# Attention with memory and a feed-forward stage on one core: the second group's maxima ahead of the block transpositions, phi behind the scalings, the next pair's fourth scores between two parts of the values

## The chip, the core and the metric

The kernel runs on one core of a Trainium2 chip. The metric is device time in microseconds (us). A core has engines that run side by side, each working through its own instructions in order: PE (TensorE) multiplies matrices (PEld is its loading of weights), DVE (VectorE), ACT (ScalarE) and POOL (GpSimd) work on elements, and SP issues most of the DMA transfers. PE has two clock levels, 1.2 and 2.4 GHz; the profile shows the granted level as a share of the full one.

## What is computed

```python
B, H, S, D = (4, 8, 576, 64)
scores = scale * np.matmul(q, k.transpose(0, 1, 3, 2))      # scale = 1/8
scores = np.where(causal, -1000000000.0, scores)
a = np.exp(scores - scores.max(-1, keepdims=True))
a /= a.sum(-1, keepdims=True) + 1e-09
local = np.matmul(a, v)
phi = lambda x: np.where(x > 0, x, np.exp(x) - 1.0) + 1.0
mem_out = einsum('bhsd,bhde->bhse', phi(q), M_prev) / (einsum('bhsd,bhd->bhs', phi(q), z_prev)[..., None] + 1e-06)
attn = g * mem_out + (1 - g) * local                         # g = sigmoid(beta), per head
x = attn.transpose(0, 2, 1, 3).reshape(B * S, H * D)         # 2304 x 512
h = x @ w_in                                                 # 512 x 2048
out = (h * sigmoid(1.702 * h)) @ w_out                       # 2048 x 512
```

All in float32. A product of the feed-forward stage is made of three passes of split numbers (high times high, low times high, high times low).

## The kernel before, in words

**Attention goes by pairs.** A pair is one batch and two heads; there are 16. The first four (batch 0) go through `plan_rest`, the other twelve through `plan_full`. Below they are full pairs 1 to 12. The change touches the full pairs, but for one line that also holds for the four.

**A full pair, in the order in which PE meets it.** The 576 rows of queries are four row blocks of 128 (i = 0 to 3) and a tail of 64. PE does, for one pair: the *fourth scores* (i = 3, four matmuls of 512 columns, tile `ps`, two PSUM banks); the *second group* (i = 2, 1, 0, tile `rows`, four banks); then the scores of the tail of the *next* pair together with the *early part* of the values (tile `po`, four banks: memory product from `qpt`, and keys from block 8 on); then the *late part* of the values (key blocks 0 to 7), behind which the fourth scores of the next pair stand. The four banks of `rows` and of `po` are the same PSUM: the early part cannot start before the last exponential has read `rows`, and the second group cannot start before the last subtraction `xl` has read `po`.

**Softmax of one row block.** DVE adds the mask and finds the maximum (line 642, called *maxima*; a second short instruction reads the accumulator), ACT does the exponential with its row sums (line 649, tile `a`), DVE adds the sums and takes the reciprocal (lines 732 and 733), POOL scales the rows (line 652), DVE transposes the block in 32 x 32 pieces into `eT` (line 860; the tail at lines 868 and 869). The early part waits for the transpositions of i = 3 and 2, the late part for those of i = 1 and 0.

**phi(q).** ACT makes exp of the negative part (lines 562 and 569), POOL takes the positive part and adds (line 577 and a tensor_tensor at helper line 168), multiplies with z (`qmt`), DVE sums (`nrm`, line 592) and takes the reciprocal, POOL multiplies (`qp<-qp,nrm`), DVE transposes (line 612, `qpt`, called *query transposition*). phi is made one pair ahead; its tile `qp` has one buffer, so the next phi waits for the query transposition.

**Values into the next stage.** ACT copies `po` into `xh`, DVE subtracts into `xl` (both at helper lines).

**Feed-forward blocks fill PE.** The first product is 128 blocks of twelve matmuls (tile `pm`, 256 or 320 columns, two PSUM banks in turn). ACT copies a finished block out (`hk`, line 160) and SP stores it to DRAM; a block can start only when its bank has been copied out. The second product (tile `acc`, line 1274) follows after all pairs.

**What sets the order.** `at(slot, prio, fn)` puts an emission into a slot with a priority, `feed` and `PACE` hand out blocks between, and a scheduler that simulates the time at build makes each engine's order from that. `tc.add_manual_dep(..., NOSYNC, ...)` only fixes an order on one engine; with SYNC it is a wait. `group` keeps its matmuls together and lets the first wait for what its list names. `behind_x` orders an instruction behind the last `xl`. `decode` puts one unpacking of output weights (three DVE instructions, lines 1102, 1103 and 1105, *bit operations*, behind one ACT scaling, line 1120) into most full pairs.

## Time and profile before

| | |
|---|---|
| median of 3 runs | 624.48 us (622.62 to 630.42) |
| profiled execution, its own time | 625.55 us |
| its span, first to last instruction | 623.8 us |
| mean granted clock of PE | 0.978 |
| busy: PE, DVE, ACT, POOL | 90%, 67%, 55%, 39% of the span |

PE is busy for nine tenths of the span, so the time is PE's work plus PE's idle time. The idle time lies at the start, where the first inputs arrive, and in the stretch of the pairs; from 400 us on PE is busy throughout. Of an engine that is not PE, only that idle time counts that PE waits for.

### The profile page before, as it was taken

How to read it: one execution, taken by the hardware profiler on the slowest of the kernel's cores; microseconds unless marked ns; L12 is line 12 of the kernel's file. 1: busy time of each engine (PE TensorE's matmuls, PEld its weight loads, DVE VectorE, ACT ScalarE, POOL GpSimd, SP SyncE). 2: the span in 40 equal slices, each digit the busy share in tenths (PEclk: the TensorE clock that was granted, in tenths of full speed). 3: DMA queues.
4: the chain of work that ended last, by engine and by line, in shares of the span. 5: the costliest groups of instructions: out<-in, count | busy, mean ns of one | idle time of the engine just before them, and what ended most of it. 6: DMA issues, size and time to landing. Idle time of an engine off the chain costs nothing.

```text
span 623.8 us, 17375 instructions
## 1 busy us (share of the span) xinstructions
PE 559.6 (90%) x6984; PEld 497.3 (80%) x6984; DVE 417.1 (67%) x993; ACT 343.1 (55%) x816; POOL 244.8 (39%) x326
## 2 busy tenths in 40 slices
PE   5799998987699787988898898799999999999997
PEld 4367776866577676876777798799999999999997
DVE  5788876647766555665755735957588569756964
ACT  5678785445535444464544523655676865666441
POOL 4757575557446337247346340240402301320000
PEclk9999999989989899999998999899999999999999
DMA  7976444545654554655642564422545823562002
GB/s 250 369 275 205 134 135 149 179 139 165 208 170 120 202 149 160 204 162 159 208 142 78 178 199 165 154 90 96 191 140 138 272 73 79 164 189 76 25 1 77
DMA packets 48736, 97.73 MB, mean 157 GB/s; under 512 B 5520, under 2 KB 33424, under 8 KB 48656
## 3 DMA queue, kind: packets, MB, share of 16 engines
q1 hardware_dynamic: 42416, 74.60, 37.1%
q0 software_dynamic: 6240, 22.02, 11.4%
q8 instruction: 55, 0.90, 0.6%
q14 instruction: 25, 0.20, 0.1%
HBM read 73.01 MB, written 23.59 MB: 155 GB/s over the span
## 4 chain that ended last, share of the span: by engine, by line
PE 33%; issue 10%; DVE 9%; POOL 4%; DMA 4%; ACT 3%; POOLq 0%; ACTq 0%; DVEq 0%
PE acc L1274 15%; PE pm L141 11%; PE po L141 5%; POOL g L1217 2%; DMA g<-gd 2%; DMA wraw<-in_w_out_dram 2%; PE ps L141 2%; POOL a L652 2%; DVE eT L860 1%; ACT a L649 1%; DVE ps L642 1%; DVE xl L168 1%; DVE rows L642 1%; DVE g L168 1%; DVE eT L868 1%
## 5 line engine op out<-in xcount | busy, mean ns | idle before, releaser
L141 PE MATMUL pm<-xh,wi 128*128 128x320 f32 (+1 forms) x1024 | 220.6, 309 | 19.9 <-ACT hk L160 16.2
L141 PEld LDWEIGHTS pm<-xh,wi 128*128 128x128 f32 x1024 | 169.5, 195 | 39.1 <-ACT hk L160 19.4
L1274 PE MATMUL acc<-oh,wo 128*128 128x384 f32 x672 | 169.9, 337 | 0.2 <-ACT oh L160 0.2
L141 PE MATMUL pm<-xl,wi 128*128 128x256 f32 (+1 forms) x512 | 154.0, 301 | 0.6 <-DVE xl L168 0.6
L1274 PEld LDWEIGHTS acc<-oh,wo 128*128 128x128 f32 x672 | 121.8, 188 | 0.5 <-ACT oh L160 0.5
L1274 PE MATMUL acc<-ol,wo 128*128 128x384 f32 x336 | 111.4, 338 | 0.2 <-DVE ol L168 0.2
L168 DVE TENSOR_TENSOR ol<-g,oh 128x768 fp32r<-128x768 f32 x84 | 79.9, 956 | 44.4 <-ACT oh L160 44.0
L141 PEld LDWEIGHTS pm<-xl,wi 128*128 128x128 f32 x512 | 99.9, 195 | 0.9 <-DVE xl L168 0.9
L160 ACT ACTIVATE oh<-g 128x768 fp32r<-128x768 f32 x84 | 69.9, 842 | 48.6 <-PE acc L1274 41.6
L652 POOL TENSOR_SCALAR a<-a,sm,g 128x512 f32<-128x512 f32 (+3 forms) x112 | 69.2, 629 | 44.5 <-DVE sm L733 34.0
L1217 POOL DMA_DIRECT2D g<-gd x48 | 34.8, 725 | 111.7 <-DVE ol L168 65.5
L160 ACT ACTIVATE hk<-pm 128x256 f32<-128x256 f32 (+1 forms) x113 | 45.5, 409 | 59.8 <-PE pm L141 47.4
L1274 PEld LDWEIGHTS acc<-ol,wo 128*128 128x128 f32 x336 | 63.0, 188 | 0.5 <-DVE ol L168 0.5
L141 PE MATMUL po<-eT,vr 32*64 32x64 f32 (+4 forms) x3072 | 53.5, 258 | 6.9 <-issue 6.9
L649 ACT ACTIVATE a<-rows,nm 128x256 f32<-128x256 f32 (+2 forms) x72 | 33.2, 473 | 45.2 <-DVE nm L642 33.4
L141 PE MATMUL ps<-kqf 64*64 64x512 f32 (+3 forms) x288 | 39.5, 547 | 20.1 <-DVE sm L733 13.8
L141 PEld LDWEIGHTS po<-eT,vr 32*64 32x64 f32 x3072 | 48.6, 136 | 10.2 <-issue 9.7
L860 DVE STREAM_TRANSPOSE eT<-a 128x1024 f32<-128x1024 f32 (+3 forms) x48 | 40.5, 843 | 18.4 <-POOL a L652 17.4
L168 POOL TENSOR_TENSOR qp<-qp,nrm 128x576 f32<-128x576 f32 (+1 forms) x16 | 17.2, 1074 | 85.2 <-DVE sm L733 83.6
L642 DVE CUSTOM_DVE_ANT_0 ps<-ps,mask 128x512 f32<-128x512 f32 (+3 forms) x72 | 38.1, 556 | 17.2 <-PE ps L141 16.4
L1223 ACT ACTIVATE g<-g 128x768 f32<-128x768 f32 x48 | 39.5, 838 | 13.6 <-DMA g<-gd 13.2
L168 DVE TENSOR_TENSOR g<-g,g 128x768 f32<-128x768 f32 x48 | 45.5, 953 | 1.4 <-ACT g L1223 1.4
(146 smaller groups left out, 750.2 us busy)
## 6 DMA issues: line engine op xcount, KB each, us to landing
g<-gd POOLq DMA_DIRECT2D x48, 384.0 KB, 4.8
vr<-in_vt_dram SPq DMA_DIRECT2D x24, 576.0 KB, 5.0
gd<-hk SPq DMA_DIRECT2D x64, 160.0 KB, 2.3
kqf<-in_kq_dram SPq DMA_DIRECT2D x12, 768.0 KB, 5.0
wraw<-in_w_in_dram SPq DMA_DIRECT2D x16, 512.0 KB, 5.7
gd<-hk SPq DMA_DIRECT2D x64, 128.0 KB, 2.0
wraw<-in_w_out_dram SPq DMA_DIRECT2D x10, 512.0 KB, 4.1
qr<-in_qt_dram SPq DMA_DIRECT2D x12, 288.0 KB, 3.1
```

The costliest lines, as they stand in the source:

```text
L141: x = nc.tensor.matmul(out, l, r, start=start, stop=stop)
L160: return nc.scalar.activation(out=dst, in_=src, func=AF.Copy, **kw)
L168: return (nc.vector if eng == "V" else nc.gpsimd).tensor_tensor(out=dst, in0=a, in1=b, op=op)
L642: x = nc.vector.tensor_tensor_reduce(out=ps, in0=ps, in1=mk, op0=ALU.add, op1=ALU.min, scale=-0.125, scalar=1e38 if j == 0 else nm[:, j - ...
L649: return nc.scalar.activation(out=a, in_=ps, func=AF.Exp, scale=-1.0, bias=nm, accum_out=sm)
L652: return (nc.vector if eng == "V" else nc.gpsimd).tensor_scalar(out=a, in0=a, scalar1=r, scalar2=gcol, op0=ALU.mult, op1=ALU.mult)
L860: x = nc.vector.transpose(out=blocks()[:, :4 * i + 4, i:9 - i:8 - 2 * i].rearrange("p k h n -> p h k n"), in_=U["a", i].rearrange("p h (k ...
L868: behind_x(nc.vector.transpose(out=e[:, :, 4], in_=a[:, :16]))
L1217: x = nc.gpsimd.dma_start(t, gd[4 * kh + p][:, :, t0:t0 + QN].rearrange("i p t -> p i t"))
L1223: x = nc.scalar.activation(out=t, in_=t, func=AF.Gelu_apprx_sigmoid)
L1274: nc.tensor.matmul(acc[b, j][:, :QN], W[2 * p + kk][:, WPART[i], sp, 128 * j:128 * j + 128], mv[:, kk], start=first and p + kk == 0 and sp ...
```

## The change

Five edits. (1) `a_blocks`: the transposition of i = 3 now stands on DVE behind the second group's maxima (`state["max"]`) and behind the reciprocal that was emitted last (`state["inv"]`), and those of i = 2, 1, 0 two slots later, behind the last reciprocal; they were in slots of their own, behind `xl` alone. (2) `qblocks`: the query transposition comes behind a reciprocal too. (3) `qphi`: POOL's positive part comes behind the last scaling emitted. (4) `products`: the late part is split into key blocks 4 to 7 and 0 to 3, and `first_group` puts the next pair's fourth scores between the two. (5) `exp_unit`: the exponentials of i = 3 stand on ACT behind the copy `xh`.

```diff
--- before.py
+++ after.py
@@ -574,7 +574,8 @@
             if rest:
                 nc.vector.scalar_tensor_tensor(out=qp, in0=qv(), scalar=0.0, in1=qm, op0=ALU.max, op1=ALU.add)
             else:
-                nc.gpsimd.tensor_scalar(out=qp, in0=qv(), scalar1=0.0, scalar2=None, op0=ALU.max)
+                x = nc.gpsimd.tensor_scalar(out=qp, in0=qv(), scalar1=0.0, scalar2=None, op0=ALU.max)
+                tc.add_manual_dep(x.ins, state["scaled"], NOSYNC, reason="not yet")
                 tt("P", qp, qp, qm, ALU.add)
 
         def zmul():
@@ -609,9 +610,11 @@
 
         def qblocks():
             t = P["qT"] = att.tile([128, 2, 9, 32], F32, name="qpt0", bufs=2)
-            P["qblocks"] = nc.vector.transpose(
+            x = nc.vector.transpose(
                 out=t.rearrange("p k s n -> p s k n"),
-                in_=P["qp"][:, :9].rearrange("p s (k n) -> p s k n", n=32)).ins.name
+                in_=P["qp"][:, :9].rearrange("p s (k n) -> p s k n", n=32))
+            tc.add_manual_dep(x.ins, state["inv"], NOSYNC, reason="not yet")
+            P["qblocks"] = x.ins.name
 
         steps = (qmin, qexp, qphi, zmul, norm, smul)
         if rest:
@@ -622,7 +625,7 @@
         else:
             times = (7, 7, 8, 9, 10, 11)
             at(s0 + 11, 53, mplain)
-            at(s0 + 12, 53, qblocks)
+            at(s0 + 12, 89.6, qblocks)
         for k, fn in zip(times, steps):
             at(s0 + k, 49 if fn is zmul else 53, fn)
         if p + 1 < len(pairs):
@@ -725,16 +728,19 @@
             used(U.get(("in", h, i), U["ps", h, i]), x)
             if i < 2:
                 behind_hk(x)
+            if i == 3 and "xh" in state:
+                tc.add_manual_dep(x.ins, state["xh"], NOSYNC, reason="not yet")
             U["exp", h, i] = state["exp"] = state["late A"] = x.ins.name
 
         def inv_unit(i):
             sm = U["rs", i] = sml.tile([128, 2], F32, name="sm")
             nc.vector.tensor_reduce(out=sm, in_=U["sm", i], op=ALU.add, axis=AX.X)
-            nc.vector.reciprocal(out=sm, in_=sm)
+            state["inv"] = nc.vector.reciprocal(out=sm, in_=sm).ins.name
 
         def scale_unit(h, i):
             hh = 2 * c + h
-            scale_rows(U["a", i][:, h], U["rs", i][:, h:h + 1], g1[:, hh:hh + 1])
+            x = scale_rows(U["a", i][:, h], U["rs", i][:, h:h + 1], g1[:, hh:hh + 1])
+            state["scaled"] = x.ins.name
 
         return max_unit, exp_unit, inv_unit, scale_unit
 
@@ -860,7 +866,8 @@
             x = nc.vector.transpose(
                 out=blocks()[:, :4 * i + 4, i:9 - i:8 - 2 * i].rearrange("p k h n -> p h k n"),
                 in_=U["a", i].rearrange("p h (k n) -> p h k n", n=32))
-            behind_x(x)
+            tc.add_manual_dep(x.ins, state["max"], NOSYNC, reason="not yet")
+            tc.add_manual_dep(x.ins, state["inv"], NOSYNC, reason="not yet")
             P["tr", i] = x.ins.name
 
         def t_blocks():
@@ -877,7 +884,7 @@
 
         def products():
             po, ms, ops = U["po"], P["ms"], []
-            for k in (-2, -1, *range(8, KB), *range(8)):
+            for k in (-2, -1, *range(8, KB), *range(4, 8), *range(4)):
                 for Q in range(4):
                     for h in range(2):
                         r, own = slice(32 * Q, 32 * Q + 32), h == Q // 2
@@ -893,9 +900,9 @@
                             ops.append((k, Q, h, i, 4 + own, w, slots(P["eT"], r, k, h, i, own)))
             last = {o[1:3]: n for n, o in enumerate(ops)}
 
-            def part(early):
+            def part(*ks):
                 for n, (k, Q, h, x, y, l, mv) in enumerate(ops):
-                    if early == (k < 0 or k >= 8):
+                    if k in ks:
                         dst = po[64 * h:64 * h + 64, Q, 32 * x:32 * y].rearrange("p (s n) -> p s n", n=32)
                         mm(dst, l, mv, k == -2, last[Q, h] == n)
                 state["pe"] += 0.5
@@ -921,7 +928,7 @@
                         parts.append((r, slice(256, CT), po[r, 2 * h:2 * h + 2, 128:160]))
                 for r, x, src in parts:
                     xh, xl = [t[r, c, x].rearrange("p (s n) -> p s n", s=src.shape[1]) for t in xq[n]]
-                    copy("A", xh, src)
+                    state["xh"] = copy("A", xh, src).ins.name
                     subs.append((xl, src, f32(xh)))
                 if c == NP - 1:
                     xplan[n] = state["slot"] + 1
@@ -943,15 +950,16 @@
                 fns.append(lambda: s_tail(p + 1, prep[p + 1]["tail"]))
             room()
             part = products()
-            group(fns + [lambda: part(True)], names)
-            values["next"] = (lambda: None, [lambda: part(False)], [P["tr", 1]])
+            group(fns + [lambda: part(-2, -1, *range(8, KB))], names)
+            values["next"] = (lambda: None, [lambda: part(*range(4, 8)), lambda: part(*range(4))], [P["tr", 1]])
 
         def first_group():
             late = values.pop("next", None)
             names, fns = (late[2], late[1]) if late else (rooms(KEEP), [])
             for h in range(2):
                 U["ps", h, 3] = U["in", h, 3] = bank("ps")
-            group(fns + [lambda: s_quads(p, 3, [U["ps", h, 3] for h in range(2)])], names)
+            fns.insert(1, lambda: s_quads(p, 3, [U["ps", h, 3] for h in range(2)]))
+            group(fns, names)
 
         def second_group():
             own = late_ps["rows"] = ExitStack()
@@ -980,7 +988,7 @@
                 at(x, (30, 29, 26, 25)[i], lambda h=h, i=i: exp_unit(h, i))
                 at(x + 1, 13 - i, lambda h=h, i=i: scale_unit(h, i))
             at(x, 91 - i, lambda i=i: inv_unit(i))
-            at(k0 + k + 3, 13 - i, lambda i=i: a_blocks(i))
+            at(k0 + (4 if i == 3 else 6), (18, 17, 16, 89.4)[i], lambda i=i: a_blocks(i))
         at(k0 + 7, 40, early_values)
         at(k0 + 7, 99, lambda: feed(1.0, True))
         if p + 1 == len(pairs):
```

Line numbers of the changed kernel are 1 to 8 higher from line 577 on (642 becomes 645, 652 becomes 655, 860 becomes 866).

On DVE, in full pair 9, from the reciprocal of i = 3 on (`rows` with 384, 256 and 128 columns are the maxima of i = 2, 1, 0; `eT<-a3` is the transposition of i = 3; `qpt0` that of the queries), before:

```order
L733 RECIPROCAL sm_4537<-sm_4537 128x2
L612 STREAM_TRANSPOSE qpt0_4648<-qp_4509 128x9x2x32
L860 STREAM_TRANSPOSE eT_4542<-a3_4531 128x2x16x32
L642 ISA rows_4578,nm_4619<-rows_4578,mask_145 128x384
L642 ISA nm_4619 128x1
L642 ISA rows_4579,nm_4621<-rows_4579,mask_145 128x384
L642 ISA nm_4621 128x1
L642 ISA rows_4580,nm_4623<-rows_4580,mask_145 128x256
```

and now, where the maxima of i = 2 follow the same reciprocal directly:

```order
L738 RECIPROCAL sm_4521<-sm_4521 128x2
L645 ISA rows_4548,nm_4589<-rows_4548,mask_145 128x384
L645 ISA nm_4589 128x1
...
L738 RECIPROCAL sm_4615<-sm_4615 128x2
L866 STREAM_TRANSPOSE eT_4526<-a3_4515 128x2x16x32
L613 STREAM_TRANSPOSE qpt0_4619<-qp_4493 128x9x2x32
L737 TENSOR_REDUCE sm_4621<-sum3_164 128x2
L738 RECIPROCAL sm_4621<-sm_4621 128x2
L737 TENSOR_REDUCE sm_4624<-sum4_165 128x2
L738 RECIPROCAL sm_4624<-sm_4624 128x2
L866 STREAM_TRANSPOSE eT_4526<-a2_4601 128x2x12x32
```

Both transpositions moved behind all six maxima, and the transposition of i = 2 behind the last two reciprocals. Before, the query transposition stood ahead of the maxima of i = 2 in ten of the twelve full pairs, and the transposition of i = 3 in seven of them (pairs 1, 5, 7 and 9 to 12) and between the maxima of i = 2 and 1 or 0 in the other five; now neither stands ahead of the maxima of i = 2 in any.

On POOL, in the same pair (`a3` and `a2` are scalings, `qp<-qr` is the positive part), before:

```order
L652 TENSOR_SCALAR a3_4531<-a3_4531,sm_4537,g1_158 128x512 x2
L577 TENSOR_SCALAR qp_4897<-qr_4233 128x576
L652 TENSOR_SCALAR a2_4631<-a2_4631,sm_4650,g1_158 128x384 x2
L652 TENSOR_SCALAR a2_4643<-a2_4643,sm_4653,g1_158 128x256 x2
L652 TENSOR_SCALAR a2_4643<-a2_4643,sm_4656,g1_158 128x128 x2
L168 TENSOR_TENSOR qp_4897<-qp_4897,qmt_181 128x576
```

and now:

```order
L655 TENSOR_SCALAR a2_4601<-a2_4601,sm_4615,g1_158 128x384 x2
L655 TENSOR_SCALAR a2_4610<-a2_4610,sm_4621,g1_158 128x256 x2
L655 TENSOR_SCALAR a2_4610<-a2_4610,sm_4624,g1_158 128x128 x2
L577 TENSOR_SCALAR qp_4881<-qr_4203 128x576
L168 TENSOR_TENSOR qp_4881<-qp_4881,qmt_181 128x576
L168 TENSOR_TENSOR qmt_181<-qp_4881,zb_4516 128x2x4x64
```

The positive part moved from ahead of six scalings to behind them.

On PE the scheduler also deals the blocks out anew. Matmuls of blocks (twelve to a block) that stand in each full pair between the late part with its fourth scores and the second group (A), and between the second group and the next tail scores (B), of 256 columns unless marked w (320 columns), as the order of the changed kernel has them:

| pair | 2 | 3 | 4 | 5 | 6 | 7 | 8 | 9 | 10 | 11 | 12 |
|---|---|---|---|---|---|---|---|---|---|---|---|
| A | 12w | 12w | 12w | 24 | 24 | 24 | 12w | 12w | 12 | 24 | 12 + 12w |
| B | 27w | 33w | 24w | 48 | 51 | 45w | 42w | 42w | 54 | 45 | 36w |

Between the early and the late part stand 0 to 18 matmuls of blocks in each pair, before and now. Over the twelve pairs 36 matmuls of 320 columns (three blocks) fewer stand among the pairs than before, and 36 more behind the last pair.

## Rows read from the trace of the kernel before

**Rows 1.** Stretches by time: busy us and count per engine, clock, DMA share, GB/s
```profile
104.00:362.00 258.00, 219.53 (x4494) 184.54 (x4491) 159.94 (x521) 122.87 (x398) 130.06 (x172) 0.95 0.53 164
362.00:443.00 81.00, 74.97 (x760) 73.64 (x745) 52.33 (x97) 38.79 (x73) 16.36 (x15) 0.98 0.41 140
```

**Rows 2.** PE's waits, 104 to 362 us: total us, times, longest
```profile
PE ps L141 <- DVE sm L733: 13.8, 5, 4.6
PE pm L141 <- ACT hk L160: 10.7, 10, 3.0
PE po L141 <- issue: 6.9, 6, 2.1
PE ps L141 <- issue: 2.9, 1, 2.9
PE rows L141 <- DVE xl L168: 1.9, 3, 0.6
PE ps L141 <- ACT hk L160: 1.4, 1, 1.4
```

**Rows 3.** The six stretches at half clock: sum of busy time, same columns
```profile
sum 23.88, PE 13.76 PEld 11.01 DVE 14.40 ACT 15.39 POOL 14.36; mean PE 2.29 PEld 1.83 DVE 2.40 ACT 2.57 POOL 2.39
```

**Rows 4.** Timeline of PE, full pair 9: start, us, instruction, [idle before]
```profile
273.31 2.27 PE L141 MATMUL po<-eT,vr 32*64 32x160 f32 x128
275.50 1.09 PE L141 MATMUL ps<-kqf 64*64 64x512 f32 x8
280.24 1.53 PE L141 MATMUL rows<-kqf 64*64 64x384 f32 x24
...
287.03 0.50 PE L141 MATMUL pm<-xh,wi 128*128 128x256 f32 x2 [1.56 <-ACT hk L160]
...
289.91 0.77 PE L141 MATMUL ps<-kqf 64*64 64x256 f32 x8
```

**Rows 5.** Timeline of DVE, full pair 9
```profile
275.63 0.69 DVE L1105 SCALAR_TENSOR_TENSOR r<-wraw,r 128x512 int32<-128x512 int32 x1
...
276.64 0.70 DVE L642 CUSTOM_DVE_ANT_0 ps<-ps,mask 128x512 f32<-128x512 f32 x1 [0.17 <-PE ps L141]
...
280.57 0.11 DVE L733 RECIPROCAL sm<-sm 128x2 f32<-128x2 f32 x1
281.93 0.78 DVE L612 STREAM_TRANSPOSE qpt<-qp 128x576 f32<-128x576 f32 x1 [1.25 <-POOL qp L168]
283.43 1.25 DVE L860 STREAM_TRANSPOSE eT<-a 128x1024 f32<-128x1024 f32 x1 [0.72 <-POOL a L652]
284.70 0.57 DVE L642 CUSTOM_DVE_ANT_0 rows<-rows,mask 128x384 f32<-128x384 f32 x1
...
287.16 0.17 DVE L733 RECIPROCAL sm<-sm 128x2 f32<-128x2 f32 x1
...
288.83 0.98 DVE L860 STREAM_TRANSPOSE eT<-a 128x768 f32<-128x768 f32 x1 [0.39 <-POOL a L652]
```

**Rows 6.** Timeline of ACT, full pair 9
```profile
285.42 0.58 ACT L649 ACTIVATE a<-rows,nm 128x384 f32<-128x384 f32 x1 [4.64 <-DVE nm L642]
...
286.55 0.43 ACT L160 ACTIVATE hk<-pm 128x320 f32<-128x320 f32 x1
```

**Rows 7.** Timeline of POOL, full pair 9
```profile
280.74 1.15 POOL L168 TENSOR_TENSOR qp<-qp,nrm 128x576 f32<-128x576 f32 x1 [7.15 <-DVE sm L733]
...
283.36 1.65 POOL L577 TENSOR_SCALAR qp<-qr 128x576 f32<-128x576 f32 x1
```

**Rows 8.** Instructions on `pm` alone in two stretches, columns as above (no POOL)
```profile
276.52:280.24 3.72, 3.72 (x24) 3.52 (x24) 0.00 (x0) 0.43 (x1) 1.00 0.96 293
298.66:303.87 5.21, 4.48 (x36) 4.26 (x36) 0.00 (x0) 0.77 (x2) 1.00 0.89 280
```

**Rows 9.** Timeline of DVE and of POOL, full pair 4: first bit operation, product with z
```profile
173.99 1.41 DVE L1102 TENSOR_SCALAR r<-r 128x512 int32<-128x512 int32 x1
...
173.83 1.28 POOL L168 TENSOR_TENSOR qmt<-qp,zb 128x512 f32<-128x512 f32 x1
```

## The prediction

> **What bounds the kernel now.** I read the stretches by time first. Between 104 and 362 us, while the twelve full pairs run, PE is busy for 219.5 of 258.0 us; between 362 and 443 us it idles 6.0 us [rows 1]. The stretch of the pairs is where the change acts, and there the other engines have room (DVE 160 us, POOL 130 us of 258), so what counts is PE's 38.5 us of idle time and what its clock costs.
>
> PE's waits in that stretch name the places [rows 2]. 13.8 + 1.4 = 15.2 us stand ahead of the tail scores, that is, PE waits until the early part may start. 10.7 us are blocks that wait for a PSUM bank which ACT has not copied out. 1.9 us are the second group, waiting for `xl`. 9.8 us carry no releaser (6.9 + 2.9, "issue"). The clock comes on top: in six stretches it was granted at half, 1.2 instead of 2.4 GHz, and PE worked for 13.76 of their 23.88 us [rows 3]; half of that, 6.9 us, is lost.
>
> The timeline of pair 9 shows how both large waits arise [rows 4 to 6]. The second group runs on PE at 280.24 and DVE is free at 280.68. But the query transposition comes next on DVE, waits 1.25 us for POOL, then the transposition of i = 3 waits 0.72 us for POOL, and the maxima of i = 2 start only at 284.70. So ACT stands still for 4.64 us; the block's copy `hk` is queued behind the exponentials of i = 2 and ends at 286.98, and PE, which had filled both banks, waits 1.56 us until 287.03. The same lateness goes on through exponential, scaling and transposition of i = 2 to the tail scores at 289.91.
>
> **The change part by part.** No instruction is added or removed; all have their old size. So I work out when things become ready, counting from the start s of the late part.
>
> *When the maxima of i = 2 can start.* Late part and fourth scores take 3.2 us on PE, 273.31 to 276.52 [rows 4, 8]. With the fourth scores in the middle they end about 1.15 us earlier, at s + 2.1. But DVE has the bit operations ahead of these maxima; they end at 276.32 = s + 3.0 [rows 5], since they hang on an ACT scaling that the change leaves where it is. So in pairs 4 to 12 the maxima of i = 3 start at s + 3.05 instead of s + 3.33, and only in pairs 2 and 3, without bit operations, at s + 2.25. From there to the reciprocal of i = 3 DVE takes 276.64 to 280.68 = 4.04 us [rows 5], plus the small transposition of the tail, 64 columns, which now comes behind the maxima: 0.24 on the line through 0.78 for 576 columns and 1.25 for 1024 [rows 5]. Together 4.3. The maxima of i = 2 are ready at s + 7.35 (s + 6.55 in pairs 2 and 3). Before, in pair 9, it was s + 11.39. That exponential i = 3 comes behind `xh` on ACT costs nothing: its scaling is due only after the reciprocal 4 us later.
>
> *From these maxima to the tail scores.* The six maxima with their reciprocal take 284.70 to 287.33 = 2.63 us; then the transposition of i = 3 (1.25, its scaling done by then), the query transposition (0.78), four small sums and reciprocals (0.5), the transposition of i = 2 (0.98) [rows 5], 0.1 between them and 0.23 to PE: 6.5 us. That is longer than pair 9's 5.2, since the two transpositions now lie inside. So the tail scores are ready at s + 13.85 (s + 13.05), where pair 9 had s + 16.6. Bounds: 5.2, if the two transpositions hide under waits as they do there, to 7.5, if POOL or ACT are late by 1 us; I take 6.5, the sum of durations.
>
> *What PE has to do in that time.* 3.2 us as above, 1.45 for the second group (280.24 to 281.69), and the blocks of columns A and B: 3.72/24 = 0.155 us for a matmul of 320 columns, 4.48/36 = 0.125 for one of 256 [rows 8]. Pair by pair from 2 to 12 the sums are 10.7, 11.6, 10.2, 13.7, 14.0, 14.6, 13.0, 13.0, 12.9, 13.3, 13.6 us. What is missing to the ready times is idle: 2.35, 1.45, 3.65, 0.15, 0, 0, 0.85, 0.85, 0.95, 0.55, 0.25 = 11.0 us. In pair 1 the query transposition used to be done before, and now lies in the chain: about 2.2 us instead of 1.4. Together 13.2 us, against 15.2 + 1.9 before (waits for `xl` are inside the sums). **Gain 3.9 us.**
>
> *The blocks' banks.* With the exponentials of i = 2 no longer late, the copy behind them ends about 2.3 us after those maxima start (0.72 to the exponentials, 1.13 for them, 0.43 for the copy, [rows 5, 6]), while PE is still in the second block after the second group. In one or two pairs with 256-column blocks the copies behind the last exponentials may hold PE for half a microsecond; I leave 1.4 us. **Gain 9.3 us.** Pair 9 alone shows 1.56 us of it in one wait [rows 4].
>
> *phi on POOL.* It leaves the 1.65 us ahead of the scalings and delays the product with z by as much. The wait that it can cause is that of `nrm` on DVE, ahead of the maxima of i = 2. POOL had been idle 7.15 us when it next worked for phi [rows 7], so this cover holds. The loads on SP that reuse phi's input tiles go out some 2 to 3 us later, with the stores of copied blocks queued behind; they have a whole pair of time.
>
> *Clock.* Of six gaps with half clock behind them three shrink under 1 us; 1.15 us each, from 6.9/6: **gain 2.3 us**, hedged for the one that the long waits of pairs 1, 2 and 4 may add.
>
> *Left as they are:* the 9.8 us without a releaser (PE's own supply of instructions or something else that the profile does not show) and the 6.0 us behind the pairs. The order of copies and weight conversions on ACT changes there too, three blocks come to it, and I allow 3 us either way.
>
> **Sum.** 3.9 + 9.3 + 2.3 = 15.5 us from the profiled execution's 625.55 gives 610.0. That execution was 1.1 us above the median, so I predict 609.0.
>
> **Rivals.**
>
> *The bit operations are stretched.* With phi later, the product with z and the scaling of the tail on POOL run 1.65 us later, closer to the bit operations. In pair 4 the first of these took 1.41 us beside POOL's product with z [rows 9]; a later one in pair 9, with two inputs, took 0.69 [rows 5]. If 1 us comes so into every pair's chain, the ready time is s + 14.85, the idle times of pairs 4 to 12 grow by 7 us, with one more slow-clock stretch: 617. By my count the two meet only in pairs 5 to 7, with no or few blocks between early and late part, and PE is the later one there. The Trainium skill has this as a rule ("SBUF — State Buffer", section "Who interferes with whom"): a VectorE tensor_scalar in its two-port mode, or a VectorE instruction with two SBUF inputs, and a GpSimd instruction exclude each other for the whole instruction. The pair 4 row agrees with it.
>
> *The stall only moves.* The blocks no longer wait, but PE arrives earlier at the tail scores and waits there: if the chain is 7.5 instead of 6.5 us in all pairs, idle is 11 us more and the clock gains nothing, 609 + 11 + 2 = 622, no change that can be told. For it: this wait is the largest class already [rows 2], though in five of the twelve pairs the maxima of i = 2 stood ahead of the transposition of i = 3. Against it: what I count is gained ahead of those maxima, 4 us in pair 9.
>
> *More is gained.* The waits without releaser fall where small matmuls follow each other closely; with the fourth scores between them half could go, and the chain could be 5.5 us (idle 6 us less): 600.
>
> *Slower.* DVE works in order, and `nrm` stands ahead of the maxima of i = 2. If POOL's later phi made `nrm` late, all pairs would wait for it. It decides only once the product with z is more than 7.15 - 1.65 = 5.5 us later than now; at 5.5 + 2.6 us the cost is 12 x 2.6 = 31 us, the 15.5 gained are gone twice, and the time is 640.
>
> That DVE does not do what the edits say is excluded by its order.
>
> **How the numbers follow.** Forecast (602 to 614) 0.50; stretched bit operations 0.16; the stall only moves 0.16; more gained 0.13; slower 0.05. The range from 599 to 622 leaves out the slower case and the ends of the last two gains; the likeliest case alone has 602 to 614. About 2% is what a measurement of this kernel can tell from no change, 612.0 and 637.0 us. Below 612 lie most of the forecast (0.42), the larger gain (0.13) and little of the rest: 0.56. Slower 0.04, the rest 0.40.
>
> **What would show it.** Right: the exponentials of i = 2 start within 2 us behind the second group's matmuls; PE's waits for `hk` fall from 10.7 to 1 or 2 us; tail scores come about 13.9 us behind the late part in pairs 4 to 12, and PE still waits for them in pairs 1 to 4. Wrong: waits ahead of the tail scores of over 20 us in sum (chain longer than 7 us), bit operations of over 1 us in most pairs, POOL's phi ending behind DVE's need, or idle time between 362 and 443 us far from 6 us.

## The result and the profile after

The changed kernel takes **595.91 us** (median; 595.68 to 599.34) against 625.92 for the kernel before in the same comparison: a ratio of **0.953, 95% interval 0.946 to 0.960**. The prediction was 609.0 us with a range of 599 to 622. The direction was right; the gain is 30 us where 15.5 was worked out, and the time lies below the range.

The stretches by time first (us, busy time and count of PE, PEld, DVE, ACT, POOL, then clock, DMA share, GB/s). I cut both kernels at the same events: the second group of the first full pair, the end of the last values, the first matmul of the second product. Kernel before:

```profile
102.50:368.70 266.20, 227.73 (x4774) 191.68 (x4774) 162.29 (x524) 124.75 (x403) 132.69 (x176) 0.96 0.54 166
368.70:442.50 73.80, 67.77 (x480) 66.84 (x481) 50.76 (x95) 37.12 (x69) 13.91 (x11) 0.98 0.37 128
```

Changed kernel:

```profile
103.70:339.40 235.70, 215.79 (x4738) 179.69 (x4737) 164.50 (x526) 124.09 (x399) 135.61 (x177) 0.98 0.59 189
339.40:413.10 73.70, 71.08 (x517) 70.68 (x517) 51.78 (x94) 37.50 (x71) 13.22 (x10) 1.00 0.40 132
```

All of the gain lies in the stretch of the pairs: 266.2 us became 235.7. PE's idle time there fell from 38.5 to 19.9 us. Its busy time fell as well, by 12 us; the 36 matmuls that now stand behind the last pair are about half of that (36 x 0.155 = 5.6 us, [rows 8]), the rest is the clock. The second stretch kept its length with those 36 matmuls more in it.

PE's waits in the pairs, changed kernel (us in total, times, longest), to be read beside [rows 2]:

```profile
PE po L141 <- issue: 7.3, 5, 2.6
PE rows L141 <- DVE xl L168: 2.6, 6, 0.7
PE ps L141 <- ACT r L1128: 2.4, 1, 2.4
PE ps L141 <- ACT qmt L569: 2.0, 1, 2.0
PE pm L141 <- ACT hk L160: 1.9, 1, 1.9
PE ps L141 <- ACT hk L160: 1.7, 1, 1.7
```

The three rows of `ps` are the waits ahead of the tail scores (the releasers named had long been done; what PE waits for is the last transposition). They are 6.1 us now, where [rows 2] had 15.2. The block waits `pm <- hk` fell from 10.7 to 1.9 us. The waits without a releaser stayed.

Full pair 9, the pair of [rows 4 to 7]. PE:

```profile
252.56 1.21 PE L141 MATMUL po<-eT,vr 32*64 32x128 f32 x64
253.69 1.09 PE L141 MATMUL ps<-kqf 64*64 64x512 f32 x8
254.71 1.37 PE L141 MATMUL po<-eT,vr 32*64 32x160 f32 x64
258.40 1.53 PE L141 MATMUL rows<-kqf 64*64 64x384 f32 x24 [0.37 <-DVE xl L168]
266.21 0.77 PE L141 MATMUL ps<-kqf 64*64 64x256 f32 x8
```

DVE in the same pair (the maxima of i = 3, `xl`, the tail transposition, the first maxima of i = 2, the transposition of i = 3, that of the queries, that of i = 2):

```profile
255.51 0.69 DVE L645 CUSTOM_DVE_ANT_0 ps<-ps,mask 128x512 f32<-128x512 f32 x1
...
257.14 1.12 DVE L168 TENSOR_TENSOR xl<-po,xh 128x256 fp32r<-128x256 f32 x4
258.29 0.71 DVE L875 STREAM_TRANSPOSE eT<-at 128x512 f32<-128x512 f32 x1
...
259.95 0.57 DVE L645 CUSTOM_DVE_ANT_0 rows<-rows,mask 128x384 f32<-128x384 f32 x1
...
262.67 1.25 DVE L866 STREAM_TRANSPOSE eT<-a 128x1024 f32<-128x1024 f32 x1
263.83 0.73 DVE L613 STREAM_TRANSPOSE qpt<-qp 128x576 f32<-128x576 f32 x1
...
264.98 0.96 DVE L866 STREAM_TRANSPOSE eT<-a 128x768 f32<-128x768 f32 x1
```

ACT in the same pair (the copy `xh`, the first exponential of i = 2, the block copy behind it):

```profile
256.12 0.99 ACT L160 ACTIVATE xh<-po 128x256 fp32r<-128x256 f32 x4 [2.44 <-PE po L141]
...
260.67 0.58 ACT L652 ACTIVATE a<-rows,nm 128x384 f32<-128x384 f32 x1 [1.19 <-DVE nm L645]
...
261.92 0.44 ACT L160 ACTIVATE hk<-pm 128x320 f32<-128x320 f32 x1
```

The maxima of i = 2 start at 259.95, which is s + 7.39 counted from the start of the late part (252.56); before it was s + 11.39. ACT waits 1.19 us ahead of the exponentials of i = 2 where it waited 4.64 [rows 6]. Neither the transposition of i = 3 nor that of the queries makes DVE wait for POOL any more. The transposition of i = 2 ends at 265.94, before PE asks for it: the tail scores start at 266.21 without a wait.

Over the whole stretch of the pairs, DVE's waits for POOL ahead of its transpositions, before and then in the changed kernel (where the query transposition has none):

```profile
DVE eT L860 <- POOL a L652: 17.4, 26, 1.5
...
DVE qpt L612 <- POOL qp L168: 11.2, 9, 1.2
```

```profile
DVE eT L866 <- POOL a L655: 1.3, 8, 0.2
```

Not in every pair did the start of these maxima move. In pairs 2 and 3 they started at s + 7.44 and s + 7.38 before the change already, since both transpositions stood between the maxima there and not ahead of them. DVE in full pair 2 before (s = 114.10; first maxima of i = 2, query transposition, first maxima of i = 1, transposition of i = 3 ahead of the maxima of i = 0):

```profile
121.54 0.57 DVE L642 CUSTOM_DVE_ANT_0 rows<-rows,mask 128x384 f32<-128x384 f32 x1
...
122.76 0.78 DVE L612 STREAM_TRANSPOSE qpt<-qp 128x576 f32<-128x576 f32 x1
123.46 0.40 DVE L642 CUSTOM_DVE_ANT_0 rows<-rows,mask 128x256 f32<-128x256 f32 x1
...
124.27 1.25 DVE L860 STREAM_TRANSPOSE eT<-a 128x1024 f32<-128x1024 f32 x1
```

With both behind the last maxima the tail scores of pair 2 come at s + 13.48 instead of s + 14.80.

**The time taken apart.** In each profile below I split the stretch from the first full pair's second group to the first matmul of the second product: PE's gaps by what they stand ahead of, the clock's loss (half of PE's busy time while half clock was granted), and what is left, PE's work at full clock.

| us | stretch | tail scores | second group | block copies | issue | behind pairs | idle in all | clock loss | work |
|---|---|---|---|---|---|---|---|---|---|
| before | 340.0 | 15.2 | 1.9 | 10.9 | 10.6 | 6.0 | 44.5 | 12.9 | 282.6 |
| changed | 309.5 | 6.1 | 2.6 | 1.9 | 9.3 | 2.6 | 22.5 | 5.1 | 281.8 |
| w_dve | 343.9 | 12.4 | 2.6 | 15.5 | 9.4 | 6.1 | 45.9 | 12.9 | 285.1 |
| w_split | 307.2 | 8.4 | 1.9 | 0.4 | 5.3 | 5.0 | 21.0 | 5.1 | 281.1 |
| w_phi | 314.2 | 6.1 | 2.6 | 1.9 | 9.6 | 3.4 | 23.7 | 8.4 | 282.0 |
| w_xh | 329.8 | 6.7 | 16.3 | 2.2 | 7.2 | 4.3 | 36.7 | 10.2 | 283.0 |
| o_dve | 310.3 | 9.5 | 1.9 | 0.4 | 7.9 | 4.1 | 23.7 | 5.1 | 281.5 |
| o_tr | 332.0 | 13.0 | 1.9 | 1.9 | 15.0 | 4.2 | 35.9 | 13.8 | 282.4 |
| o_qb | 330.9 | 13.7 | 1.9 | 12.5 | 7.2 | 5.8 | 41.2 | 6.1 | 283.7 |
| x_hk | 352.5 | 18.7 | 1.9 | 8.9 | 12.6 | 5.9 | 48.0 | 25.1 | 279.4 |
| after_again | 310.8 | 7.2 | 2.6 | 1.9 | 7.2 | 4.7 | 23.5 | 4.9 | 282.4 |
| b1 | 308.2 | 6.3 | 2.6 | 1.0 | 7.4 | 4.1 | 21.3 | 5.1 | 281.8 |
| b13 | 306.3 | 5.2 | 2.6 | 0 | 5.1 | 6.0 | 18.9 | 5.0 | 282.4 |
| b13p202 | 304.0 | 6.5 | 1.1 | 0 | 6.7 | 2.0 | 16.3 | 6.6 | 281.1 |

In b1, b13 and b13p202, where the tail scores have a group of their own, the column "tail scores" holds the waits ahead of the early part. The clock loss is an estimate: in the stretch from 398.64 to 402.06 us before, at a granted clock of 0.50, matmuls of 256 columns followed each other at 0.213 us, behind it at 0.12 us, so a little less than half is lost. The last column stays within 279 to 285 us in all of them. So a difference between these kernels of more than these 6 us is idle time plus clock, and it can be read off a row. Two profiles of the same kernel (changed, after_again) differ by 2 us in "issue" and in "behind pairs" each; differences of that size in these columns say nothing.

### The profile page after: what moved, and what is told of

The parts are those of the page before. It is cut to its first block, busy times and chain, and to the rows that moved or that the text cites. A ratio compares the mean times of both kernels' runs of the same rounds, so it can differ in the third digit from the quotient of the medians.

```text
span 593.9 us, 17375 instructions
## 1 busy us (share of the span) xinstructions
PE 551.4 (93%) x6984; PEld 489.5 (82%) x6984; DVE 419.3 (71%) x994; ACT 343.2 (58%) x815; POOL 245.4 (41%) x326
## 3 DMA queue, kind: packets, MB, share of 16 engines
q0 software_dynamic: 6240, 22.02, 12.2%
## 5 line engine op out<-in xcount | busy, mean ns | idle before, releaser
L141 PE MATMUL pm<-xh,wi 128*128 128x320 f32 (+1 forms) x1024 | 213.0, 301 | 6.3 <-ACT hk L160 3.8
L141 PEld LDWEIGHTS pm<-xh,wi 128*128 128x128 f32 x1024 | 164.3, 189 | 17.7 <-issue 6.5
L141 PE MATMUL pm<-xl,wi 128*128 128x256 f32 (+1 forms) x512 | 150.7, 295 | 0.8 <-issue 0.4
L141 PEld LDWEIGHTS pm<-xl,wi 128*128 128x128 f32 x512 | 96.9, 190 | 0.5 <-DVE xl L168 0.5
L141 PEld LDWEIGHTS po<-eT,vr 32*64 32x64 f32 x3072 | 47.8, 134 | 20.0 <-issue 11.4
L141 PE MATMUL po<-eT,vr 32*64 32x64 f32 (+4 forms) x3072 | 55.8, 257 | 7.5 <-issue 7.3
L168 POOL TENSOR_TENSOR qp<-qp,nrm 128x576 f32<-128x576 f32 (+1 forms) x16 | 17.1, 1072 | 73.1 <-DVE sm L738 69.2
L652 ACT ACTIVATE a<-rows,nm 128x384 f32<-128x384 f32 (+2 forms) x72 | 33.2, 474 | 15.8 <-DVE nm L645 15.5
```

The source lines that it names most:

```text
L141: x = nc.tensor.matmul(out, l, r, start=start, stop=stop)
L168: return (nc.vector if eng == "V" else nc.gpsimd).tensor_tensor(out=dst, in0=a, in1=b, op=op)
L652: return nc.scalar.activation(out=a, in_=ps, func=AF.Exp, scale=-1.0, bias=nm, accum_out=sm)
```

## Experiments

Theory A: the order on DVE (edits 1 and 2) carries the gain, since the exponentials of i = 2, the block copies queued behind them on ACT and the last transposition all hang on the second group's maxima. Theory B: the fourth scores in the middle of the values and the blocks dealt anew (edit 4) carry it. PE's order of blocks follows edit 4 alone: kernels with it have the changed kernel's order among the pairs, kernels without it that of before.

### One edit taken out of the changed kernel at a time

**w_dve: without edits 1 and 2.**

```diff
-            tc.add_manual_dep(x.ins, state["inv"], NOSYNC, reason="not yet")
-            at(s0 + 12, 89.6, qblocks)
+            at(s0 + 12, 53, qblocks)
...
-            tc.add_manual_dep(x.ins, state["max"], NOSYNC, reason="not yet")
-            tc.add_manual_dep(x.ins, state["inv"], NOSYNC, reason="not yet")
+            behind_x(x)
...
-            at(k0 + (4 if i == 3 else 6), (18, 17, 16, 89.4)[i], lambda i=i: a_blocks(i))
+            at(k0 + k + 3, 13 - i, lambda i=i: a_blocks(i))
```

> The changed kernel without edits (1) and (2): the block and query transpositions stand on DVE where they stood before, PE's order of blocks is that of the changed kernel. Theory A (the order on DVE carries the gain, since ACT's exponentials and with them the block copies hang on the second group's maxima): PE's waits for hk come back to 8 to 11 us and those ahead of the tail scores to 10 or more, with them the half-clock stretches: 613 to 622 us. Theory B (the fourth scores in the middle of the values and the blocks dealt anew carry it): 597 to 604 us, hk waits under 4 us.

Measured: 630.76 us, ratio to the kernel before 1.013 (1.009 to 1.017). PE's waits in the pairs:

```profile
PE pm L141 <- ACT hk L160: 15.5, 13, 2.6
...
PE ps L141 <- ACT qmt L562: 5.4, 2, 3.2
PE ps L141 <- ACT hk L160: 4.0, 1, 4.0
```

The other three edits by themselves make the kernel slower than before, by 7 us and beyond the 613 to 622 that theory A expected. Theory B is out. The block waits are larger than before the change (15.5 against 10.7), with transpositions among and ahead of the maxima again.

**w_split: without edit 4.**

```diff
-            for k in (-2, -1, *range(8, KB), *range(4, 8), *range(4)):
+            for k in (-2, -1, *range(8, KB), *range(8)):
...
-            fns.insert(1, lambda: s_quads(p, 3, [U["ps", h, 3] for h in range(2)]))
-            group(fns, names)
+            group(fns + [lambda: s_quads(p, 3, [U["ps", h, 3] for h in range(2)])], names)
```

> The changed kernel without edit (4): late part in one piece, fourth scores behind it, and PE's order of blocks among the pairs that of the kernel before; DVE's order as changed. Theory A: 596 to 602 us, waits for hk 1 to 3 us, those ahead of the tail scores at most 4 us above the changed kernel's (maxima of i = 3 about 1 us later). Theory B: 612 to 622 us, most of the waits of the kernel before back.

Measured: 595.41 us, ratio 0.957 (0.952 to 0.962), as fast as the changed kernel. The split and the new dealing of blocks bring nothing that can be measured. The reason stands in DVE's timeline: in full pair 3 of this kernel the maxima of i = 2 start at s + 7.39, and so they do in five pairs of the changed kernel, pair 9 among them. With the split the maxima of i = 3 come earlier (s + 2.95 instead of s + 3.31), but `xl` stands between them and the maxima of i = 2; it needs the copy `xh` and that needs the end of the late part, which the split moves from s + 2.3 to s + 3.5. `xl` starts at s + 4.58 either way.

**w_phi: without edit 3.**

```diff
-                tc.add_manual_dep(x.ins, state["scaled"], NOSYNC, reason="not yet")
```

> The changed kernel without edit (3): POOL's positive part of phi (1.65 us) again ahead of scalings. Theory A (phi only costs where a scaling waits behind it and PE has no cover): 596 to 601 us. Rival C (each pair's chain from the scalings to the tail scores is the bound, so 1.65 us comes into all twelve pairs, and slow clock behind some): 608 to 616 us.

Measured: 596.28 us, ratio 0.957 (0.952 to 0.962). No difference to the changed kernel; rival C is out. Its profile has the same waits ahead of the tail scores, 6.1 us.

**w_xh: without edit 5.**

```diff
-            if i == 3 and "xh" in state:
-                tc.add_manual_dep(x.ins, state["xh"], NOSYNC, reason="not yet")
```

> The changed kernel without edit (5): exponentials of i = 3 may stand ahead of the copy xh on ACT. Theory A (no engine waits for it): 594 to 598 us. Rival D (the copy xh then ends late, xl and the second group with it, by 1 us in each pair): 600 to 608 us, waits of the second group for xl of 6 us or more instead of 2.6.

Measured: 613.66 us, ratio 0.986 (0.982 to 0.991). My theory expected no effect; rival D was right, and the effect is larger than it said. PE's largest wait in the pairs, then ACT and DVE in full pair 9 (the first exponential of i = 3, `xh`, `xl`), where the late part ends at 268.59:

```profile
PE rows L141 <- DVE xl L168: 16.2, 9, 2.8
```

```profile
268.79 0.69 ACT L652 ACTIVATE a<-ps,nm 128x512 f32<-128x512 f32 x1 [2.62 <-DVE nm L645]
...
270.71 0.97 ACT L160 ACTIVATE xh<-po 128x256 fp32r<-128x256 f32 x4
```

```profile
271.71 1.12 DVE L168 TENSOR_TENSOR xl<-po,xh 128x256 fp32r<-128x256 f32 x4 [0.93 <-ACT xh L160]
```

With the fourth scores in the middle, the exponentials of i = 3 are ready before the late part has ended, and the scheduler puts them ahead of `xh`. ACT is then busy with them until 270.7, `xh` comes 2 us late, `xl` with it, and PE waits for `xl` at the second group. Before the change the scheduler had put `xh` first by itself, in every full pair from the second on. So edit 5 is a guard for edit 4: without the one the other costs 18 us, with it nothing that can be measured.

### One edit alone on the kernel before

**o_dve: edits 1 and 2.** The diff of w_dve the other way round, on the kernel before.

> The kernel before with edits (1) and (2) alone: both transpositions behind the second group's maxima on DVE, nothing else changed; PE's order of blocks is that of before. Theory A (these two edits carry the whole gain): 592 to 600 us, idle time of PE between the first second group and the last value as in the changed kernel, under 22 us. Rival B (phi's new place or the guard of the copy is needed as well): 604 to 616 us.

Measured: 596.77 us, ratio 0.957 (0.949 to 0.965). The two edits on DVE give the whole gain, with PE's order of before. Rival B of this run is out.

**o_tr: edit 1 alone**, the transposition of i = 3 (and those of i = 2, 1, 0) moved, the query transposition left.

> The kernel before with edit (1) alone: the transposition of i = 3 behind the maxima, the query transposition ahead of the maxima of i = 2 in all twelve pairs (ten before). Theory A1 (each of the two transpositions costs its wait for POOL plus its own time, in pair 9 2.0 us each): about half of the gain, 605 to 615 us, block waits 3 to 7 us. Rival A2 (the transposition of i = 3, whose scaling stands behind the others on POOL, is what makes the maxima late): 593 to 602 us. Rival A3 (the query transposition is): 618 to 626 us.

Measured: 619.56 us, ratio 0.996 (0.992 to 0.999).

**o_qb: edit 2 alone**, the query transposition moved, the others left.

> The kernel before with edit (2) alone: the query transposition behind the maxima, the transposition of i = 3 ahead of the maxima of i = 2 in six pairs and among the maxima in the other six. Theory A1: 605 to 615 us. Rival A2: 618 to 626 us. Rival A3: 593 to 602 us.

Measured: 615.98 us, ratio 0.988 (0.980 to 0.996). PE's two largest waits in the pairs of o_qb:

```profile
PE pm L141 <- ACT hk L160: 12.4, 10, 2.6
PE ps L141 <- DVE sm L735: 10.1, 4, 4.3
```

Alone they bring 3 and 7 us, together 26. All three theories on the split between them fall; A1 was nearest with o_qb only. Both transpositions stood in one queue ahead of the same maxima, and each waited for POOL: with one gone, the other still holds them. In o_tr the maxima of i = 2 start at s + 9.40 in most pairs where PE arrives early (the query transposition at s + 8.6 is ahead); in o_qb between s + 11.4 and s + 12.5 in five pairs and between s + 7.4 and s + 9.1 in the rest. By the table, o_tr has rid itself of the block waits (1.9 us), not of the tail waits (13.0) nor of the clock's loss (13.8); o_qb the other way round on the clock (6.1), with 12.5 us of block waits. o_tr's row also holds 15.0 us of issue waits, two of them over 4 us, which no edit explains.

### Are the block waits a cost of their own?

**x_hk: the kernel before, with one block copy moved ahead of the exponentials of i = 2.**

```diff
-            if i < 2:
+            if i < 3 and p >= MB * NP:
+                behind_hk(x)
+            elif i < 2:
                 behind_hk(x)
...
-                at(x, (30, 29, 26, 25)[i], lambda h=h, i=i: exp_unit(h, i))
+                at(x, (30, 29, 28.5, 25)[i], lambda h=h, i=i: exp_unit(h, i))
```

> The kernel before with one edit that the change does not have: on ACT the copy of the block that follows the second group stands ahead of the exponentials of i = 2 in the full pairs, not behind; DVE keeps its order but for small sums. Theory P (the blocks' waits are a cost of their own, as the prediction's sum had them): PE's waits for hk fall from 10.7 to at most 3 us and those ahead of the tail scores stay at 15 us: 612 to 617 us. Rival S (both waits are one lateness: PE reaches the tail scores earlier and waits there): hk waits fall to at most 3 us, those ahead of the tail scores rise by 6 to 10 us: 620 to 627 us.

Measured: 637.1 us, ratio 1.022 (1.014 to 1.029). Neither theory had it. ACT in full pair 9 (the block copy, the first exponential of i = 2, the next copies), and PE behind it:

```profile
291.40 0.44 ACT L160 ACTIVATE hk<-pm 128x320 f32<-128x320 f32 x1 [2.97 <-PE pm L141]
291.73 0.58 ACT L649 ACTIVATE a<-rows,nm 128x384 f32<-128x384 f32 x1
...
295.60 0.72 ACT L160 ACTIVATE hk<-pm 128x320 f32<-128x320 f32 x2
```

```profile
296.10 0.50 PE L141 MATMUL pm<-xh,wi 128*128 128x256 f32 x2 [1.56 <-ACT hk L160]
```

The exponentials now also wait for the block: the maxima of i = 2 begin at 290.38, the exponential only at 291.73, behind the copy. The next two copies stand behind all exponentials, and PE waits 1.56 us there, as long as in [rows 4], one block later. Block waits fell to 8.9 us, tail waits rose to 18.7. The larger part of the loss is the clock: 25.1 us against 12.9 with nearly the same idle time (48.0 and 44.5); five of its gaps are over 3.2 us, two in the kernel before.

This run does not isolate the copy, though. The expectation says that DVE keeps its order but for small sums, and in the trace it does not. In pair 9 the transposition of i = 3 now stands behind the maxima of i = 2, so that these start at s + 9.40 and not at s + 11.39; and the place of a transposition among the maxima changed in pairs 2, 3, 4, 8 and 12 as well, in pairs 2 and 8 to ahead of those of i = 2. So x_hk shows that putting this copy first brought no gain. That the block copies are late only because the maxima are agrees with o_dve, whose edits touch DVE alone and whose block waits are 0.4 us; no run here moves the copies alone.

### Towards a faster version

The same kernel as the changed one was run beside three others built on it.

**after_again.**

> The changed kernel once more, as the measure for the three kernels beside it on the same chip: 593 to 599 us; PE's idle time and the clock's loss in the pairs and behind them as in its first profile (22.5 and 5.1 us) within 3 us each.

Measured: 595.22 us, ratio 0.951 (0.946 to 0.955); idle 23.5 us, clock 4.9.

**b1: the tail scores in a group of their own.**

```diff
-                names += rooms(0)
...
-                fns.append(lambda: s_tail(p + 1, prep[p + 1]["tail"]))
+                group([lambda: s_tail(p + 1, prep[p + 1]["tail"])], rooms(0))
+                state["pe"] -= 0.3
...
-            group(fns + [lambda: part(-2, -1, *range(8, KB))], names)
+            group([lambda: part(-2, -1, *range(8, KB))], names)
```

> The changed kernel with the next pair's tail scores in a group of their own that waits only for its PSUM banks, ahead of the early part, which keeps its waits. Theory T (6.1 us of PE's idle time ahead of the tail scores in pairs 1, 2 and 4 are waits for the last transposition, and the 0.77 us of these scores fit into them): about 2 us less, 592 to 595.5 us. Rival U (the banks come free no earlier, or the scores' results block ACT or DVE behind them): 596 us or more.

Measured: 595.77 us, ratio 0.951 (0.947 to 0.955): no gain, and a time between the ranges of the two theories. PE now waits ahead of the early part, behind the tail scores. The waits in pairs 1 and 2 did shrink (1.69 to 1.15, 1.95 to 1.47 us), that of pair 4 grew from 2.39 to 2.95; in all 0.9 us less, too little to be told.

**b13: also the sums of i = 2 and the query transposition behind all six maxima.**

```diff
+            tc.add_manual_dep(x.ins, state["max"], NOSYNC, reason="not yet")
...
-            nc.vector.tensor_reduce(out=sm, in_=U["sm", i], op=ALU.add, axis=AX.X)
+            x = nc.vector.tensor_reduce(out=sm, in_=U["sm", i], op=ALU.add, axis=AX.X)
+            if i < 3 and p >= MB * NP:
+                tc.add_manual_dep(x.ins, state["max"], NOSYNC, reason="not yet")
```

> As the kernel before it in this list, and the sums of i = 2 with the query transposition stand behind all six maxima on DVE in every pair (in the changed kernel they stand between them in full pair 10, where PE then waits 1.88 us for a block's copy and runs at half clock behind it). Theory V (the wait and the slow clock go with the order): 2 to 4 us less than the kernel before it in this list, waits for hk under 0.5 us, 589 to 593 us. Rival W (the clock falls at another gap instead): no difference over 1 us.

Measured: 591.95 us, ratio 0.945 (0.942 to 0.949), 3.8 us less than b1 (590.24 to 593.19 against 592.85 to 597.57). Time and block waits are as theory V had them. In the changed kernel the edits order the query transposition behind a reciprocal, not behind the maxima, and in full pair 10 the scheduler put both between the maxima of i = 2 and those of i = 1. DVE, ACT and PE of the changed kernel there:

```profile
281.10 0.16 DVE L737 TENSOR_REDUCE sm<-sum 128x2 f32<-128x4 f32 x1 [0.84 <-ACT a L652]
...
281.37 0.76 DVE L613 STREAM_TRANSPOSE qpt<-qp 128x576 f32<-128x576 f32 x1
282.06 0.40 DVE L645 CUSTOM_DVE_ANT_0 rows<-rows,mask 128x256 f32<-128x256 f32 x1
```

```profile
283.23 0.47 ACT L652 ACTIVATE a<-rows,nm 128x256 f32<-128x256 f32 x1 [1.89 <-DVE nm L645]
```

```profile
285.27 0.50 PE L141 MATMUL pm<-xh,wi 128*128 128x256 f32 x2 [1.88 <-ACT hk L160]
```

It is the old stall in small: a small sum waits 0.84 us for ACT, the transposition follows, ACT waits 1.89 us for the maxima of i = 1, the block copy stands behind their exponentials, and PE waits 1.88 us, with half clock from 286.44 on. In b13 the block waits are gone. By the table the clock's loss is the same as in b1, so of the gain only the idle time (2.4 us) is accounted for by that profile; that the slow clock goes with the wait was not shown.

**b13p202: also more blocks in the first pairs.**

```diff
-    PACE = ((36, 1.97), (67, 1.95), (9999, 2.3))
+    PACE = ((36, 1.97), (67, 2.02), (9999, 2.3))
```

> As the kernel before it in this list, with more blocks dealt into the first full pairs (pace 2.02 instead of 1.95 up to slot 67; 3 to 6 matmuls of 320 columns more in pairs 1, 2 and 4 before the tail scores, 12 fewer in pair 4's neighbour). Theory X (PE's idle time there is taken by blocks that else stand behind the last pair): 1 to 3 us less than the kernel before it in this list. Rival Y (they only displace idle time to the next pairs): no difference over 1 us.

Measured: **588.71 us**, ratio **0.939** (0.934 to 0.944), the fastest kernel here, 3.2 us below b13. Rival Y is out, but the mechanism of theory X is not what happened: in b13 and here alike 816 matmuls of blocks stand among the pairs and 516 behind the last one, so no block came from there. The edit deals the same blocks out otherwise: 3 and 6 matmuls more ahead of the tail scores in pairs 1 and 2, 3 and 12 fewer in pairs 3 and 4. The waits in pairs 1 and 2 fell to 0.71 and 0.60 us, but pair 4, now with one block less, waits 4.48 us ahead of the early part. By the table waits and clock in the pairs add up to more than in b13; what is less are the waits for `xl` (2.6 to 1.1 us) and above all the idle time behind the pairs (6.0 to 2.0 us), a column that differs by 2 us between two profiles of one kernel. So where these 3.2 us come from stays open, and the wait in pair 4 shows that a better dealing may be left.

## Why the prediction was too small, step by step

**The order as the cause: right, with one gap.** The forecast took its gain from the maxima of i = 2 coming early, and gave edits 3 and 5 no gain. It read this off pair 9; in pairs 2 and 3, where PE waited 2.78 and 3.11 us at the tail scores, those maxima were early already, and in pair 2 the gain is that the transpositions left the place between the maxima. In pair 3 it is also the new dealing: 33 matmuls of blocks instead of 27 stand ahead of the tail scores, and w_split, with the old dealing, waits 1.87 us there, the second profile of the changed kernel 1.08. o_dve shows that edits 1 and 2 are the whole of it, w_phi that edit 3 is nothing. Calling edit 5 free was right only in the full change: I looked at what waits behind the exponentials and not at `xh`, which edit 4 would otherwise have pushed back (w_xh).

**When the maxima start: right in size.** s + 7.35 was worked out for pairs 4 to 12; pair 9 has s + 7.39. For pairs 2 and 3 I had s + 6.55, from the maxima of i = 3 coming sooner; it is s + 7.39 and 7.78 (before the change s + 7.44 and 7.38), since what counts there is `xl` (w_split).

**From there to the tail scores: 6.5 us predicted, 6.1 measured** in pairs 2 and 4, where PE waits for it (s + 7.39 to s + 13.48). The sum of durations was the right choice between 5.2 and 7.5: in pair 9 DVE has hardly a pause from 257.14 to 265.94.

**The idle time that this leaves: the first failed step.** Predicted 13.2 us left of 17.1; measured 8.7 (6.1 + 2.6). Ready times were 0.4 us sooner, and PE's work before them longer: pair 9 has 13.65 us from the late part to the tail scores where I had 13.0, of which 0.37 is the wait for `xl` that I believed inside the sum and 0.25 the late part with the fourth scores inside it (3.45 us instead of 3.2). That is small, but each of pairs 8 to 12 was forecast to miss 0.25 to 0.95 us, and 0.65 + 0.4 us closes all of them. Pairs 5 to 12 have no wait at the tail scores. So the term failed in its idle time, the difference of ready time and PE's work: small errors in both, taken over many pairs. Gain 8.4 us instead of 3.9.

**The blocks' banks: right.** 1.4 us left predicted, 1.9 measured, gain 9.0 instead of 9.3. It came in one place only, pair 10, by an order that I had seen as harmless, and not behind the last exponentials of pairs with 256-column blocks.

**The clock: the second failed step, and the largest.** Predicted gain 2.3 us, measured 7.8 (12.9 to 5.1). Two things were wrong. First, I cut the six stretches of [rows 3] about 2 us too early; that group shows only their sum, so the clock column that would have told it is not to be seen. One of the six, as I cut it and as the clock's record has it, and the sum with the seventh stretch behind the pairs:

```profile
167.94:174.76 6.82, 3.31 (x95) 2.37 (x96) 4.80 (x20) 4.34 (x15) 5.45 (x8) 0.65 0.29 91
```

```profile
169.95:176.78 6.83, 5.33 (x191) 4.39 (x198) 5.70 (x14) 3.40 (x10) 5.85 (x9) 0.50 0.30 89
...
398.64:402.06 3.42, 3.42 (x18) 3.42 (x18) 2.97 (x6) 2.56 (x6) 0.00 (x0) 0.50 0.36 121
sum 27.31, PE 25.81 PEld 23.72 DVE 17.99 ACT 13.05 POOL 15.77; mean PE 3.69 PEld 3.39 DVE 2.57 ACT 1.86 POOL 2.25
```

A clock of 0.65 says that the cut took in full clock. Cut rightly, PE was busy at half clock for 25.81 us, a loss of 12.9 us instead of 6.9: my stretches had lain over the gaps ahead of the slow time and not over the slow time itself. Second, I let a third of it go. In the changed kernel three stretches are left, where seven were, one of them twice as long:

```profile
sum 10.23, PE 10.23 PEld 6.95 DVE 4.65 ACT 3.65 POOL 6.38; mean PE 3.41 PEld 2.31 DVE 1.55 ACT 1.22 POOL 2.13
```

**Issue waits: unchanged, right** (10.6 and 9.3 us by the table's cut). **Behind the pairs: 6.0 to 2.6 us**, inside neither the zero nor, by little, the 3 us that I allowed; but the second profile of the same kernel has 4.7, so much of this may not be the change.

**The sum.** 8.4 (tail scores and second group) + 9.0 + 7.8 + 1.3 (issue) + 3.4 (behind the pairs) + 0.8 (work) = 30.7 us; the stretch of the table is 30.5 us shorter (the terms are rounded). 15.5 were forecast. Of the 15 us missing, 5.5 are the clock, 4.5 the tail waits, 3.4 the part behind the pairs.

**The rivals.** Stretched bit operations exist, in two pairs out of nine, pair 5 and, by 0.3 us, pair 6. POOL and DVE in full pair 5 of the changed kernel (the place that [rows 9] counts to pair 4):

```profile
172.50 2.71 POOL L168 TENSOR_TENSOR qmt<-qp,zb 128x512 f32<-128x512 f32 x3
```

```profile
171.28 1.68 DVE L1111 SCALAR_TENSOR_TENSOR r<-wraw,r 128x512 int32<-128x512 int32 x1
...
173.00 1.64 DVE L1113 SCALAR_TENSOR_TENSOR r<-wraw,r 128x512 int32<-128x512 int32 x1
```

They take 1.7 us instead of 0.69 beside POOL's work for phi, and PE does not wait at the tail scores there. By the rule of the Trainium skill that the prediction drew on ("SBUF — State Buffer", section "Who interferes with whom"), a VectorE instruction with two SBUF inputs contends with a GpSimd instruction that reads SBUF. These rows agree with it. That the stall only moves did not happen: both waits fell together. The case "more is gained" had the right side and the wrong mechanism: the issue waits did not halve, and it held no more of the clock. The slower case needed `nrm` late; DVE's waits among the pairs show none ahead of it.

## What to carry to other kernels

Instructions that wait for a slow engine do not belong in an in-order queue ahead of the one that feeds everybody else; and where two such stand there, moving one shows almost nothing (3 and 7 us), moving both shows all (26 us), so an edit is not to be thrown away because it failed alone. An edit that only guards an order (a copy ahead of an exponential) has to be costed together with the edit that would break it. Cut a stretch of slow clock by the clock's own record and look at its clock column before a price is made of it, and price the clock as a second gain wherever long idle pieces of PE go. A test that reorders one engine under a scheduler can reorder another (x_hk): read the other engines' order before the result is put down to the edit.

## What the runs showed of the hardware

**Slow clock follows idle time, and long idle pieces are followed by it most often.** I took all of PE's gaps over 0.5 us in the stretch of the table, in its 14 profiles, and looked whether half clock was granted from 1.5 to 5.5 us after the gap had begun. Of 152 gaps under 1.5 us 9 were followed by it, of the 17 over 3.2 us all, and between these lengths both happened: in the changed kernel a gap of 1.88 us (pair 10) was followed by half clock, one of 2.39 us (pair 4) was not. So idle time and clock do not go evenly together: x_hk has 3.5 us more idle time than the kernel before, five gaps over 3.2 us where that has two, and loses 12.2 us more to the clock; o_qb has 3.3 us less idle time and loses 6.8 us less, with two such gaps as before. The lengths of the gaps alone do not decide it.

**PE's waits without a releaser** are 5 to 15 us in these profiles, mostly at the small matmuls of the values, and differed by 2.1 us between the two profiles of the changed kernel. No experiment here touched them; their cause stays open.
